# An attention and two-mixer kernel on one core: key chunks of p two per PSUM tile, two-tensor forms of small VectorE operations, q's squares on GpSimd, two score tiles for three

## The chip, the cores and the metric

The kernel runs on one core of one Trainium2 chip. The time is the device time of one execution in microseconds (us). A core has five engines with a queue of instructions each, which run in the order in which they stand: PE (TensorE: matmuls and transposes, its weight loads listed apart as PEld), DVE (VectorE), ACT (ScalarE), POOL (GpSimd) and SP (SyncE, which issues most DMAs here).

## The reference

The input goes through attention (4 batches, 12 heads, 448 tokens, head size 64) and then two mixers on x of 4 x 448 x 768. All of it is float32; the weights of the mixers come as float64.

```
def rmsnorm(x, g):
    rms = sqrt(mean(x * x, axis=-1, keepdims=True) + 1e-06)
    return x / rms * g
q_n, k_n = rmsnorm(q, g_q), rmsnorm(k, g_k)
scores = (q_n @ k_n.T) / sqrt(64)
attn = exp(scores - max(scores)); attn = attn / (sum(attn) + 1e-09)
x = attn @ v                                   # heads side by side: 768 columns
u = x + (x.T @ U @ V).T;            x = u + relu(u @ w_ch1) @ w_ch2        # first mixer
u = x + (relu(x.T @ w_tok1) @ w_tok2).T;  x = u + relu(u @ w_ch1') @ w_ch2'  # second mixer
```

## The kernel before

**Number formats.** Most matmuls split a float32 operand into a high part (fp32r, tiles named `hi`, `ph`, `gh`) and the rest (`lo`, `pl`, `gl`) and add two or three products.

**Attention, head by head.** Heads come in pairs (48 heads, 24 pairs). `load_pair` (L187) fetches q, k and v of a pair, forms the squares of q (ACT, L204) and of k (POOL, L202, by `mul`; on DVE for the first pair), sums them on DVE (L205), and gets 1/rms with a chain of small operations on 112x16 values: L206 on DVE, Ln and Exp on ACT (L208, L209), and a Newton step on DVE (L211 to L214). POOL then scales q and k (L222). Tile `sq` has one buffer, so each square waits for the sum over the one before. `turn_pair` (L233) transposes q and k on PE and splits them; twelve DMAs per pair lay out the operands of the scores.

`softmax` (L267) works on 4 chunks of 112 query rows of a head. For each chunk PE makes a score tile `sc` of 112x448 (two matmuls, one PSUM bank), DVE takes the row maximum `nm` (L276), ACT writes p = exp(sc - max) and the row sum `sm` (L278), and the score tile is free again. After every second chunk DVE adds 1e-9 to two sums (L281) and inverts them (L282), and POOL scales the two chunks of p (L285).

`weigh` (L287) needs all 4 chunks of p of a head. For each of 4 key chunks PE transposes four blocks of p into a PSUM tile `pt` (L304), ACT copies it to `ph` (L312), and DVE computes the rest `pl` (L316). PE adds the products to `pv`, and at the end DVE (with ACT for a split head) writes the result. In the first half of attention the even head of a pair is `whole`: its `ph` is plain float32, it has no `pl`, and its products are float32 matmuls. All other heads are split.

**Stages.** The first 24 heads (batches 0 and 1) run alone, with nothing but a few loads beside them: this is the lone attention. PSUM has 8 banks, and the lone attention gives 3 to `sc`, 1 to `tt` (the turned q and k), and 4 to a pool that `pt` and `pv` share (L550, L551). The other 24 heads run beside the first feed-forward part of the first mixer, with other pools. The rest of the mixers runs without attention. Along with the feed-forward parts, every weight chunk goes through `to_f32` and `split`: ACT L123, DVE L124, L125 and L129, ACT L128, POOL L132, ACT L142, POOL L143.

**What sets the order.** The code says which instruction belongs to which engine; a scheduler that works on a modelled timeline sets the order in each engine's queue when the kernel is built. A change in one stage can so reorder queues all through that stage.

Of the kernel before, what the change touches and what calls it, by code (L numbers as in the profile page):

```python
# [24 lines left out]
def attention_then_two_mixers(  # L25
# [39 lines left out]
    G = 2  # L65
    PAIRS = ((0, 1), (2, 3))

# [30 lines left out]
    pools = {"late": False}  # L98
    AT = dict(qr=2, kr=2, vr=3, qn=1, vs=2, p=8, ph=3, pl=3, sq=1)

# [86 lines left out]
    def load_pair(b, hp, whole, mul):  # L187
# [10 lines left out]
        for i, t in enumerate((qr, kr)):  # L198
            sq = pools["at"].tile([CP, 2 * NC4, D], F32, tag="sq", bufs=AT["sq"], name="sq")
            tt = t.rearrange("p h c d -> p (h c) d")  # L200
            if i:
                mul(sq, tt, tt)  # L202
            else:
                nc.scalar.activation(sq, tt, AF.Square)  # L204
            nc.vector.reduce_sum(ms[:, i], sq, axis=AX.X)  # L205
        nc.vector.tensor_scalar(ms, ms, 1.0 / D, 1e-6, op0=ALU.mult, op1=ALU.add)  # L206
        rs = pools["at"].tile([CP, 2, 8], F32, tag="rs", name="rs")
        nc.scalar.activation(rs, ms, AF.Ln)  # L208
        nc.scalar.activation(rs, rs, AF.Exp, scale=-0.5)  # L209
        nt = pools["at"].tile([CP, 2, 8], F32, tag="nt", name="nt")  # L210
        nc.vector.tensor_mul(nt, rs, rs)  # L211
        nc.vector.tensor_mul(nt, nt, ms)
        nc.vector.tensor_scalar(nt, nt, -0.5, 1.5, op0=ALU.mult, op1=ALU.add)
        nc.vector.tensor_mul(rs, rs, nt)  # L214

# [51 lines left out]
    def softmax(pr, qs, ks, kt):  # L267
        for c in range(NC4):
# [11 lines left out]
            if c % 2:  # L280
                nc.vector.tensor_scalar_add(sm, sm, 1e-9)  # L281
                nc.vector.reciprocal(sm, sm)  # L282
# [5 lines left out]
    def weigh(pr, vj, j, dst, whole):  # L288

        pv = psum("v", [P, S], "pv")  # L290

        def product(kc, ph, pl):
            if whole:
                mm(pv[:D], vj[:, kc], ph, kc == 0, kc == NC4 - 1)
                return
            vk = vj[:, kc].rearrange("p t d -> p (t d)")
            mm(pv, vk, ph, kc == 0, False)
            mm(pv, vk, pl, False, kc == NC4 - 1)

        last = None  # L300
        for kc in range(NC4):
            pt = psum("p", [CP, S], "pt")
            for c in range(NC4):
                nc.tensor.transpose(  # L304
                    pt[:, c * CP:(c + 1) * CP], pr[c][:, kc * CP:(kc + 1) * CP],
                    ident[:CP, :CP],
                )
            if last:
                product(*last)
            ph = pools["pp"].tile([CP, S], F32 if whole else F32R, tag="ph", bufs=AT["ph"],  # L310
                                  name="ph")
            nc.scalar.activation(ph, pt, AF.Copy)  # L312
            pl = None
            if not whole:
                pl = pools["pp"].tile([CP, S], F32R, tag="pl", bufs=AT["pl"], name="pl")
                nc.vector.tensor_sub(pl, pt, f(ph))  # L316
            last = kc, ph, pl
            yield
        product(*last)
# [331 lines left out]
```

## Time and profile before

| | |
|---|---|
| median of 3 runs | 1592.1 us (1589.14 to 1592.72) |
| the profiled execution | 1583.41 us, of which the span of its instructions is 1581.6 us |
| PE busy | 1496.0 us (95%) |
| DVE busy | 1192.7 us (75%) |
| ACT busy | 815.7 us (52%) |
| POOL busy | 847.2 us (54%) |
| mean granted TensorE clock | 0.988 of full speed |

The profiled execution is 8.7 us shorter than the median of the three runs. The lone attention takes about the first 200 us; the 24 heads beside the feed-forward end near 624 us; the mixers alone take the rest. In the rows below, "busy" is the time during which an engine runs at least one instruction, and an arrow `<-` behind an idle time names what ended it.

### The profile page before, as it was taken

To read this page: it belongs to the slowest core of one execution; us is meant where nothing else is said; L and a number is where in the kernel's file an instruction comes from. 1 tells how busy PE (TensorE), PEld (TensorE's weight loads), DVE (VectorE), ACT (ScalarE), POOL (GpSimd) and SP (SyncE) were. 2 spreads that over 40 slices of the span, in tenths; PEclk is the share of its full clock that TensorE was granted. 3 is DMA by queue.
4 is the path that set the end of the run, shared out by engine and by line. 5 is a ranking of instruction groups with operands and counts; after the bars stand their busy time and mean duration, and the time that the engine had idled before them with its cause. 6 is when DMAs were issued, how large, how long until landed. Compare 5 with 4: busy or idle time off the path is not lost.

```text
span 1581.6 us, 21878 instructions
## 1 busy us (share of the span) xinstructions
PE 1496.0 (95%) x7648; PEld 1303.0 (82%) x7648; DVE 1192.7 (75%) x1981; ACT 815.7 (52%) x1511; POOL 847.2 (54%) x645
## 2 busy tenths in 40 slices
PE   5999978999999999999999999999999999999998
PEld 3565566888788899898898988889999998998997
DVE  6899888988897887667858677677676676748663
ACT  5888765666566665434534345344344343524431
POOL 4667656666666554544745454455455453535540
PEclk9999979999999999999999999999999999999999
DMA  6656533445434422323314334233333332203312
GB/s 154 155 154 165 149 130 113 127 130 157 144 112 139 116 92 83 122 91 113 120 43 137 101 100 150 66 116 133 101 101 120 100 110 90 80 13 120 128 61 71
DMA packets 116046, 178.22 MB, mean 113 GB/s; under 512 B 9248, under 2 KB 105984, under 8 KB 115936
## 3 DMA queue, kind: packets, MB, share of 16 engines
q1 hardware_dynamic: 115616, 176.82, 36.7%
q8 instruction: 61, 1.00, 0.3%
q14 instruction: 49, 0.40, 0.1%
q10 hardware_dynamic: 320, 0.00, 0.0%
HBM read 135.50 MB, written 8.26 MB: 91 GB/s over the span
## 4 chain that ended last, share of the span: by engine, by line
PE 62%; DVE 12%; POOL 4%; DMA 4%; ACT 3%; issue 2%; SPq 0%; DVEq 0%; POOLq 0%; ACTq 0%
PE ps_x L77 27%; PE ps_g L77 25%; DVE w_bits L124 3%; DVE w_bits L129 2%; PE ps_u L77 2%; PE ps_t L77 2%; POOL w L143 2%; PE pv L77 2%; DMA qs<-hi 2%; DMA w_raw<-in_moe_w_ch_dram 1%; POOL w_bits L132 1%; DVE w_bits L125 1%; PE sc L77 1%; PE pt L304 1%; DVE xT L478 1%
## 5 line engine op out<-in xcount | busy, mean ns | idle before, releaser
L77 PE MATMUL ps_x<-gs,w 128*128 128x448 f32 x2592 | 566.5, 370 | 22.1 <-DVE xT L478 11.5
L77 PE MATMUL ps_g<-u,w 128*128 128x448 f32 x2592 | 546.4, 367 | 1.6 <-DVE gs L465 0.9
L77 PEld LDWEIGHTS ps_x<-gs,w 128*128 128x128 f32 x2592 | 483.4, 190 | 71.5 <-DVE xT L478 18.0
L77 PEld LDWEIGHTS ps_g<-u,w 128*128 128x128 f32 x2592 | 484.1, 188 | 42.2 <-DVE gs L465 1.5
L132 POOL TENSOR_TENSOR w_bits<-w_bits,w_round 128x768 uint32<-128x768 uint32 (+2 forms) x152 | 279.8, 1841 | 270.7 <-DVE w_bits L129 211.9
L143 POOL TENSOR_TENSOR w<-w_bits,w 128x768 fp32r<-128x768 f32 (+3 forms) x154 | 285.9, 1866 | 199.2 <-ACT w L142 198.9
L478 DVE TENSOR_TENSOR xT<-ps_x,xT 128x448 f32<-128x448 f32 x432 | 265.9, 619 | 121.4 <-PE ps_x L77 119.6
L128 ACT ACTIVATE w_round<-w_raw 128x768 uint32<-128x768 uint32 (+2 forms) x152 | 135.2, 889 | 186.2 <-POOL w_bits L132 186.0
L124 DVE TENSOR_SCALAR w_bits<-w_bits 128x768 f32<-128x768 f32 (+2 forms) x152 | 145.3, 956 | 96.0 <-ACT w_bits L123 95.9
L142 ACT ACTIVATE w<-w_bits 128x768 fp32r<-128x768 f32 (+3 forms) x154 | 124.8, 830 | 124.0 <-PE ps_x L77 68.0
L285 POOL TENSOR_SCALAR p<-p,sm 112x448 f32<-112x448 f32 x192 | 129.0, 685 | 95.3 <-DVE sm L282 49.0
L123 ACT ACTIVATE w_bits<-w_raw 128x768 f32<-128x768 f32 (+2 forms) x152 | 135.3, 891 | 85.5 <-POOL w L143 77.7
L129 DVE SCALAR_TENSOR_TENSOR w_bits<-w_raw,w_bits 128x768 uint32<-128x768 uint32 (+2 forms) x152 | 168.7, 1110 | 2.1
L278 ACT ACTIVATE p<-sc,nm 112x448 f32<-112x448 f32 x192 | 121.9, 637 | 49.8 <-DVE nm L276 41.9
L125 DVE TENSOR_SCALAR w_bits<-w_bits 128x768 uint32<-128x768 uint32 (+2 forms) x152 | 137.7, 906 | 2.9
L464 ACT ACTIVATE gs<-ps_g 128x448 fp32r<-128x448 f32 x144 | 77.8, 543 | 108.8 <-PE ps_g L77 106.1
L465 DVE SCALAR_TENSOR_TENSOR gs<-ps_g,gs 128x448 fp32r<-128x448 f32 x144 | 88.9, 619 | 52.8 <-ACT gs L464 52.5
L276 DVE TENSOR_REDUCE nm<-sc 112x1 f32<-112x448 f32 x192 | 116.3, 613 | 8.4 <-PE sc L77 7.8
L304 PEld LDWEIGHTS pt<-ident,p 112*112 112x112 f32 x768 | 86.7, 134 | 41.5 <-issue 18.5
L312 ACT ACTIVATE ph<-pt 112x448 fp32r<-112x448 f32 (+1 forms) x192 | 101.3, 546 | 30.2 <-PE pt L304 29.0
L304 PE MATMUL pt<-ident,p 112*112 112x112 f32 x768 | 111.4, 262 | 5.2 <-DVE pl L316 2.6
L387 POOL TENSOR_TENSOR u<-xT,u 128x448 fp32r<-128x448 f32 x48 | 59.1, 1248 | 65.5 <-ACT u L386 65.5
(74 smaller groups left out, 1438.4 us busy)
## 6 DMA issues: line engine op xcount, KB each, us to landing
w_raw<-in_moe_w_ch_dram SPq DMA_DIRECT2D x144, 768.0 KB, 4.4
ks<-hi SPq DMA_DIRECT2D x96, 112.0 KB, 2.4
kt<-lo SPq DMA_DIRECT2D x96, 112.0 KB, 2.3
qr<-in_q_dram SPq DMA_DIRECT2D x24, 224.0 KB, 3.1
kr<-in_k_dram SPq DMA_DIRECT2D x24, 224.0 KB, 3.2
vr<-in_v_dram SPq DMA_DIRECT2D x24, 224.0 KB, 3.1
qs<-hi SPq DMA_DIRECT2D x48, 112.0 KB, 2.8
qs<-lo SPq DMA_DIRECT2D x48, 112.0 KB, 2.7
```

What stands on the lines that cost most here:

```text
L77: nc.tensor.matmul(o, lhsT=l, rhs=r, start=start, stop=stop)
L123: nc.scalar.activation(f(w), f(high), AF.Abs)
L124: nc.vector.tensor_scalar_max(f(w), f(w), TINY)
L125: nc.vector.tensor_scalar(w, w, 3, 0x3FFFFFF8, op0=ALU.logical_shift_left, op1=ALU.bitwise_and)
L128: nc.scalar.activation(r, low, AF.Copy, scale=2.0 ** -29)
L129: nc.vector.scalar_tensor_tensor(w, high, 0xC0000000, w, op0=ALU.bitwise_and, op1=ALU.bitwise_or)
L132: nc.gpsimd.tensor_tensor(w, w, r, op=ALU.add)
L142: nc.scalar.activation(hi, w, AF.Copy)
L143: nc.gpsimd.tensor_sub(lo, w, f(hi))
L285: nc.gpsimd.tensor_scalar(x, x, sm[:, i:i + 1], 1.0, op0=ALU.mult, op1=ALU.mult)
L304: nc.tensor.transpose(pt[:, c * CP:(c + 1) * CP], pr[c][:, kc * CP:(kc + 1) * CP], ident[:CP, :CP],)
L478: nc.vector.tensor_add(xT[:, dc], px, xT[:, dc])
```

## The change

Five things change, all in attention.

- **Two key chunks per tile.** In the lone attention `weigh` turns two key chunks into one `pt` tile of two banks. One ACT copy and one DVE subtraction then cover 112x896 where there were two of 112x448. `ph` and `pl` have two buffers of double width for four of single width. Beside the feed-forward one chunk per tile remains (`turn=1`).
- **PSUM of the lone attention.** Score tiles go from 3 to 2, `pt` gets 2 tiles of two banks, and `pv` gets a bank of its own.
- **Two-tensor forms.** L206 and L281 were `tensor_scalar` with two constants or one; they become `scalar_tensor_tensor` with a constant tile (`eps`, `zeros`) as second tensor.
- **Newton step.** The operations L211 to L214 become three: the factor -0.5 goes into the first, and the addition of 1.5 into the last.
- **q's squares** are made by `mul` like k's: on POOL, for the first pair on DVE.

```diff
+    zeros = const.tile([P, 2], F32, name="zeros")
+    nc.vector.memset(zeros, 0.0)
+    eps = const.tile([P, 16], F32, name="eps")
+    nc.vector.memset(eps, 1e-6)
...
-            if i:
-                mul(sq, tt, tt)
-            else:
-                nc.scalar.activation(sq, tt, AF.Square)
+            mul(sq, tt, tt)
             nc.vector.reduce_sum(ms[:, i], sq, axis=AX.X)
-        nc.vector.tensor_scalar(ms, ms, 1.0 / D, 1e-6, op0=ALU.mult, op1=ALU.add)
-        rs = pools["at"].tile([CP, 2, 8], F32, tag="rs", name="rs")
+        ms = ms.rearrange("p a b -> p (a b)")
+        nc.vector.scalar_tensor_tensor(
+            ms, ms, 1.0 / D, eps[:CP], op0=ALU.mult, op1=ALU.add)
+        rs = pools["at"].tile([CP, 16], F32, tag="rs", name="rs")
...
-        nc.vector.tensor_mul(nt, rs, rs)
+        nc.vector.scalar_tensor_tensor(nt, rs, -0.5, rs, op0=ALU.mult, op1=ALU.mult)
         nc.vector.tensor_mul(nt, nt, ms)
-        nc.vector.tensor_scalar(nt, nt, -0.5, 1.5, op0=ALU.mult, op1=ALU.add)
-        nc.vector.tensor_mul(rs, rs, nt)
+        nc.vector.scalar_tensor_tensor(rs, nt, 1.5, rs, op0=ALU.add, op1=ALU.mult)
...
-                nc.vector.tensor_scalar_add(sm, sm, 1e-9)
+                nc.vector.scalar_tensor_tensor(
+                    sm, sm, 1e-9, zeros[:CP], op0=ALU.add, op1=ALU.add)
...
+        def product(kcs, ph, pl):
+            for i, kc in enumerate(kcs):
+                if whole:
+                    mm(pv[:D], vj[:, kc], ph[:, i], kc == 0, kc == NC4 - 1)
+                    continue
+                vk = vj[:, kc].rearrange("p t d -> p (t d)")
+                mm(pv, vk, ph[:, i], kc == 0, False)
+                mm(pv, vk, pl[:, i], False, kc == NC4 - 1)
...
+        n = AT["turn"]
+        for k0 in range(0, NC4, n):
+            kcs = range(k0, k0 + n)
+            pt = psum("p", [CP, n, BANK], "pt")[:, :, :S]
+            for i, kc in enumerate(kcs):
+                for c in range(NC4):
+                    nc.tensor.transpose(
+                        pt[:, i, c * CP:(c + 1) * CP], pr[c][:, kc * CP:(kc + 1) * CP],
+                        ident[:CP, :CP],
+                    )
             if last:
                 product(*last)
...
-        AT.update(p=12, ph=4, pl=4)
-        open_pools(inner, (("pp", 1, 0), ("s", 3, 1), ("t", 1, 1), ("p", 4, 1)))
-        pools["v"] = pools["p"]
+        AT.update(p=12, ph=2, pl=2, turn=2)
+        open_pools(inner, (("pp", 1, 0), ("s", 2, 1), ("t", 1, 1), ("p", 2, 1), ("v", 1, 1)))
...
-        AT.update(p=8, ph=3, pl=3)
+        AT.update(p=8, ph=3, pl=3, turn=1)
```

The queues change all through attention and are the same from the mixers without attention on. Three places follow. In the names, a number after a tile tells one allocation from the next; the line numbers of the changed kernel are up to 11 higher.

PE, in the middle of the lone attention, before: the transposes of the head whose chunks are p_1982, p_1999, p_2022 and p_2040, with the score matmuls and the products between them.

```order
L304 MATMUL pt_2136<-ident_67,p_1982 112x112
L304 MATMUL pt_2136<-ident_67,p_1999 112x112
L304 MATMUL pt_2136<-ident_67,p_2022 112x112
L304 MATMUL pt_2136<-ident_67,p_2040 112x112
L77 MATMUL sc_2258<-ks_2083,qs_2080 112x448
L77 MATMUL sc_2258<-kt_2086,qs_2080 112x448
L77 MATMUL sc_2351<-ks_2092,qs_2089 112x448
L77 MATMUL sc_2351<-kt_2095,qs_2089 112x448
L77 MATMUL pv_1984<-pl_2033,vs_1455 128x448
```

PE, at the like place now: the transposes of the head whose chunks are p_1861, p_1882, p_1894 and p_1918, from the first two chunks on.

```order
L314 MATMUL pt_2004<-ident_67,p_1861 112x112
L314 MATMUL pt_2004<-ident_67,p_1882 112x112
L77 MATMUL sc_2027<-ks_1755,qs_1752 112x448
L77 MATMUL sc_2027<-kt_1758,qs_1752 112x448
L77 MATMUL sc_2047<-ks_1755,qs_1752 112x448
L77 MATMUL sc_2047<-kt_1758,qs_1752 112x448
L77 MATMUL pv_1863<-pl_1911,vs_1374 128x448
L77 MATMUL pv_1863<-ph_1909,vs_1374 128x448
L77 MATMUL pv_1863<-pl_1911,vs_1374 128x448
L314 MATMUL pt_2034<-ident_67,p_1861 112x112
L314 MATMUL pt_2034<-ident_67,p_1882 112x112
```

Before, sc_2258 and sc_2351 are the last chunk of the head two further on and the first of the head after that. Now sc_2027 and sc_2047 are the third and fourth chunk of the very next head, and the head's transposes begin with its first two chunks, into both double tiles, ahead of the other two.

POOL, in the lone attention, before: the square of k between chunks of p.

```order
L222 TENSOR_TENSOR kn_2122<-kr_2100,rs_2112 112x2x4x64
L202 TENSOR_TENSOR sq_2331<-kr_2323 112x512
L285 TENSOR_SCALAR p_1945<-p_1945,sm_1939 112x448
L285 TENSOR_SCALAR p_1960<-p_1960,sm_1939 112x448
L143 TENSOR_TENSOR vs_1678<-vr_1656,vs_1678 112x4x64
L285 TENSOR_SCALAR p_1982<-p_1982,sm_1976 112x448
```

POOL, at the like place now: both squares, k's of one pair and q's of the next.

```order
L291 TENSOR_SCALAR p_1655<-p_1655,sm_1649 112x448
L291 TENSOR_SCALAR p_1676<-p_1676,sm_1649 112x448
L206 TENSOR_TENSOR sq_2183<-kr_2175 112x512
L206 TENSOR_TENSOR sq_2386<-qr_2379 112x512
L291 TENSOR_SCALAR p_1688<-p_1688,sm_1682 112x448
L148 TENSOR_TENSOR vs_1580<-vr_1559,vs_1580 112x4x64
```

A second square now stands ahead of the scaling of p_1688, and it waits for DVE's sum over the first.

## Rows read from the trace of the kernel before

**Rows 1.** Busy time by stretch: from:to, length, then each engine (instructions), clock, DMA.

```profile
core 0: us, PE busy (x) PEld busy (x) DVE busy (x) ACT busy (x) POOL busy (x), PEclk, DMA share, GB/s
39.00:188.00 149.00, 139.17 (x733) 86.96 (x732) 137.80 (x340) 123.77 (x334) 100.65 (x135) 0.99 0.62 157
203.00:624.00 421.00, 394.35 (x2101) 345.49 (x2102) 366.73 (x648) 262.42 (x535) 253.12 (x215) 0.97 0.41 121
```

**Rows 2.** Line 321, once per pair: durations, then first and last start.

```profile
L321 DVE COPY xT<-pv x12: 604/606/617, 38.6 to 197.6; 64x448 f32<-64x448 f32 x12
```

**Rows 3.** Waits of PE's weight loads, 39 to 188 us: total, times, longest.

```profile
PEld sc L77 <- ACT p L278: 6.1, 13, 0.8
PEld pv L77 <- ACT ph L312: 5.0, 9, 1.0
PEld pt L304 <- POOL p L285: 2.9, 3, 1.5
PEld sc L77 <- ACT sq L204: 2.1, 2, 1.4
```

**Rows 4.** Groups on DVE, 39 to 188 us: count | busy, mean ns | idle before.

```profile
L276 DVE TENSOR_REDUCE nm<-sc 112x1 f32<-112x448 f32 x83 | 50.0, 613 | 2.7 <-PE sc L77 2.4
L316 DVE TENSOR_TENSOR pl<-pt,ph 112x448 fp32r<-112x448 f32 x40 | 24.0, 607 | 0.0
...
L281 DVE TENSOR_SCALAR sm<-sm 112x2 f32<-112x2 f32 x41 | 10.8, 263 | 1.4 <-ACT p L278 1.3
...
L206 DVE TENSOR_SCALAR ms<-ms 112x16 f32<-112x16 f32 x13 | 5.2, 397 | 0.0
L212 DVE TENSOR_TENSOR nt<-nt,ms 112x16 f32<-112x16 f32 x12 | 4.6, 383 | 0.1
L214 DVE TENSOR_TENSOR rs<-rs,nt 112x16 f32<-112x16 f32 x12 | 4.1, 345 | 0.1
L211 DVE TENSOR_TENSOR nt<-rs 112x16 f32<-112x16 f32 x12 | 3.3, 272 | 0.3 <-ACT rs L209 0.3
L213 DVE TENSOR_SCALAR nt<-nt 112x16 f32<-112x16 f32 x12 | 3.2, 264 | 0.1
```

**Rows 5.** Groups on ACT and POOL, the same stretch.

```profile
L278 ACT ACTIVATE p<-sc,nm 112x448 f32<-112x448 f32 x83 | 52.9, 642 | 6.2 <-DVE nm L276 3.8 <-PE pt L304 1.1 <-DVE sm L282 1.1
L285 POOL TENSOR_SCALAR p<-p,sm 112x448 f32<-112x448 f32 x83 | 52.4, 646 | 28.9 <-DVE sm L282 8.2 <-ACT ph L312 7.4 <-PE pt L304 6.9
...
L312 ACT ACTIVATE ph<-pt 112x448 fp32r<-112x448 f32 x40 | 21.1, 554 | 6.0 <-PE pt L304 6.0
...
L202 POOL TENSOR_TENSOR sq<-kr 112x512 f32<-112x512 f32 x13 | 13.7, 1051 | 5.1 <-DMA kr<-in_k_dram 1.5 <-DVE ms L205 1.5 <-DVE sm L281 1.4
...
L204 ACT ACTIVATE sq<-qr 112x512 f32<-112x512 f32 x13 | 8.3, 639 | 2.7 <-DMA qr<-in_q_dram 2.6
```

**Rows 6.** The narrower evictions of 384 columns, whole execution.

```profile
L380 DVE TENSOR_TENSOR xs<-pt_x,xs 112x384 fp32r<-112x384 f32 x64 | 34.0, 550 | 13.1 <-ACT xs L379 12.9
L379 ACT ACTIVATE xs<-pt_x 112x384 fp32r<-112x384 f32 x64 | 29.9, 488 | 18.3 <-PE pt_x L372 17.8
```

**Rows 7.** DVE and POOL in order of time, near 294 and 452 us: start, length.

```profile
294.26 4.30 DVE L206 TENSOR_SCALAR ms<-ms 112x16 f32<-112x16 f32 x1
294.89 3.64 POOL L143 TENSOR_TENSOR w<-w_bits,w 128x768 fp32r<-128x768 f32 x2
...
451.19 1.36 POOL L202 TENSOR_TENSOR sq<-kr 112x512 f32<-112x512 f32 x1
451.68 3.48 DVE L129 SCALAR_TENSOR_TENSOR w_bits<-w_raw,w_bits 128x768 uint32<-128x768 uint32 x1
452.51 1.84 POOL L143 TENSOR_TENSOR w<-w_bits,w 128x768 fp32r<-128x768 f32 x1
```

**Rows 8.** The chain that ended last, two of its pieces: start, length, what.

```profile
240.31 6.32 DVE w_bits L124
...
273.33 3.62 DVE nt L213
```

More of the change, by code (lines that the diff above doesn't have):

```diff
@@ L65, in attention_then_two_mixers @@
     G = 2
-    PAIRS = ((0, 1), (2, 3))
+    BANK = 512
     const = ctx.enter_context(tc.tile_pool(name="const", bufs=1))
@@ L98, in attention_then_two_mixers @@
     pools = {"late": False}
-    AT = dict(qr=2, kr=2, vr=3, qn=1, vs=2, p=8, ph=3, pl=3, sq=1)
+    AT = dict(qr=2, kr=2, vr=3, qn=1, vs=2, p=8, ph=3, pl=3, sq=1, turn=1)
     def open_pools(stack, side):
@@ L200, in load_pair @@
             tt = t.rearrange("p h c d -> p (h c) d")
-            if i:
-                mul(sq, tt, tt)
-            else:
-                nc.scalar.activation(sq, tt, AF.Square)
+            mul(sq, tt, tt)
             nc.vector.reduce_sum(ms[:, i], sq, axis=AX.X)
-        nc.vector.tensor_scalar(ms, ms, 1.0 / D, 1e-6, op0=ALU.mult, op1=ALU.add)
-        rs = pools["at"].tile([CP, 2, 8], F32, tag="rs", name="rs")
+        ms = ms.rearrange("p a b -> p (a b)")
+        nc.vector.scalar_tensor_tensor(
+            ms, ms, 1.0 / D, eps[:CP], op0=ALU.mult, op1=ALU.add)
+        rs = pools["at"].tile([CP, 16], F32, tag="rs", name="rs")
         nc.scalar.activation(rs, ms, AF.Ln)
         nc.scalar.activation(rs, rs, AF.Exp, scale=-0.5)
-        nt = pools["at"].tile([CP, 2, 8], F32, tag="nt", name="nt")
-        nc.vector.tensor_mul(nt, rs, rs)
+        nt = pools["at"].tile([CP, 16], F32, tag="nt", name="nt")
+        nc.vector.scalar_tensor_tensor(nt, rs, -0.5, rs, op0=ALU.mult, op1=ALU.mult)
         nc.vector.tensor_mul(nt, nt, ms)
-        nc.vector.tensor_scalar(nt, nt, -0.5, 1.5, op0=ALU.mult, op1=ALU.add)
-        nc.vector.tensor_mul(rs, rs, nt)
+        nc.vector.scalar_tensor_tensor(rs, nt, 1.5, rs, op0=ALU.add, op1=ALU.mult)
+        rs = rs.rearrange("p (a b) -> p a b", a=2)
         def scale(i, shape):
@@ L290, in weigh @@
         pv = psum("v", [P, S], "pv")
[L292 to L298, printed above, removed]
-        last = None
[L301 to L307, printed above, removed]
+        def product(kcs, ph, pl):
[6 more added lines that the diff above has]
+                mm(pv, vk, pl[:, i], False, kc == NC4 - 1)
+        last = None
+        n = AT["turn"]
[8 more added lines that the diff above has]
+                    )
             if last:
                 product(*last)
-            ph = pools["pp"].tile([CP, S], F32 if whole else F32R, tag="ph", bufs=AT["ph"],
+            ph = pools["pp"].tile([CP, n, S], F32 if whole else F32R, tag="ph", bufs=AT["ph"],
                                   name="ph")
@@ L314, in weigh @@
             if not whole:
-                pl = pools["pp"].tile([CP, S], F32R, tag="pl", bufs=AT["pl"], name="pl")
+                pl = pools["pp"].tile([CP, n, S], F32R, tag="pl", bufs=AT["pl"], name="pl")
                 nc.vector.tensor_sub(pl, pt, f(ph))
-            last = kc, ph, pl
-            yield
+            last = kcs, ph, pl
+            for _ in kcs:
+                yield
         product(*last)
```

## The prediction

> **What bounds the kernel now.** I read the table of busy time by stretch first, to see which stages the edits can reach. Nothing is edited in the mixers without attention, and the queues there keep their order, so their time is taken as unchanged. Two stages remain. In the middle of the lone attention PE is busy 139.2 of 149 us and DVE 137.8; ACT has 123.8 and POOL 100.7 [rows 1]. PE and DVE are both within 8% of full, and neither alone explains the time. The line that runs once per pair of heads starts 12 times between 38.6 and 197.6 us, so a pair takes (197.6 - 38.6) / 11 = 14.45 us [rows 2]. Beside the feed-forward (421 us) PE is busy 394.4 us, that is 94%, and DVE 366.7, that is 87% [rows 1]: there PE sets the end and DVE matters where PE waits for it.
>
> Next I read what PE waits for in the lone stage. The largest waits of its weight loads are for a free score tile, 6.1 us in 13 waits behind ACT's exponential; for `ph` from ACT, 5.0 us; for p from POOL, 2.9 us; and 2.1 us behind q's square on ACT [rows 3]. So the lone stage is a chain of four engines that hand work over with little room, and what counts is both how much work DVE and ACT have and how far ahead each is.
>
> **The change part by part, lone attention.** There are 12 pairs; the first is start-up, so I count 11.
>
> *Wider `pl`.* DVE's subtraction of 448 columns takes 607 ns [rows 4], the one of 384 takes 550 ns [rows 6]. That is 57 / 64 = 0.89 ns per column, so one of 896 should take 607 + 448 x 0.89 = 1006 ns. A pair has four `pl` (one split head): 4 x 607 - 2 x 1006 = 0.42 us less on DVE. The least it can be is nothing, if the wide one takes 2 x 607.
>
> *Newton step.* The five small operations take 397 + 272 + 383 + 264 + 345 = 1661 ns per pair [rows 4]. Four at the mean of 332 take 1329: 0.33 us less. The long means are waits for POOL, shown below.
>
> *Two-tensor forms.* L281 takes 263 ns for two columns and L206 397 ns for 16 [rows 4]; nearly all of it is not work. The rows show why: at 294.26 us L206 takes 4.30 us and ends as POOL ends a pair of `w` operations that began at 294.89 and took 3.64 [rows 7]. Two-tensor forms do the same: L212 and L214 have no constant in place of a tensor and average 383 and 345 ns; at 451.68 us a scalar_tensor_tensor over SBUF takes 3.48 us behind a POOL square and a POOL subtraction in a row [rows 7]. So I count the forms at nothing. If they did help, rival C has the price.
>
> *q's squares.* ACT loses 639 ns per pair and POOL gains 1051 [rows 5]. The wider `ph`: 554 ns for 448 columns [rows 5], 488 for 384 [rows 6], so 1.03 ns per column and 1016 for 896; four wide ones for eight save 8 x 554 - 4 x 1016 = 0.37 us. ACT is relieved by 1.0 us per pair, which takes away the 2.1 us behind q's square [rows 3], and part of the 5.0. POOL goes from 100.7 to 100.7 + 10.3 x 1.05 = 111.5 of 149 us, still the least busy but in the way: more of DVE's small operations will find it running. With 7% more POOL time the waits inside the 1.33 + 2.1 us of small operations per pair grow by some 0.1 us.
>
> *Sum of the work.* DVE: 0.42 + 0.33 - 0.1 = 0.65 us per pair. PE's own idle time is 149 - 139.2 = 9.8 us, or 0.95 us per pair, so the period can follow DVE that far: 11 x 0.65 = 7 us gained. ACT's relief is counted inside this, since ACT is less full than DVE; the bound of both is PE's idle time, 11 x 0.95 = 10.5 us.
>
> *Two score tiles and a shorter lead.* This costs, and the trace has no row for two tiles. From below: nothing, if exponentials come in time. From above: the 6.1 us per 149 [rows 3] doubled, 6.1 x 159 / 149 = 6.5 us more. The order of the queue shows a second loss. Before, when PE begins to transpose a head in the second half of the stage, it has issued seven chunks of later heads; now at most two, in every head. I take a third of the upper end, 2 us, because only short waits (0.8 us at most) stand there now.
>
> *A bank of its own for `pv`.* The next head's first product waits until DVE has read the last head's `pv` (606 ns at L321 [rows 2]). In the new order a dozen transposes and two score chunks stand between, so this costs nothing; without that cover it would be 0.6 us per head.
>
> Lone attention: 7 - 2 = 5 us gained.
>
> **Beside the feed-forward.** Seven or so pairs run their small operations here. One operation fewer saves 7 x 0.33 = 2.3 us of DVE, mostly hidden under PE; q's squares add 7 x 1.05 = 7.4 us of POOL time. The long DVE waits there (L124 6.32 us, L213 3.62 us, both in the final chain [rows 8]) are meetings of two queues: L124 is not edited, and the order of POOL before it now holds one square more. L213's operation is gone, but its successors can meet POOL as well. I count 1 us of gain, with -8 to +7 for meetings that vanish or come anew.
>
> Total 6 us: 1583.4 to 1577.4 for the profiled execution. That execution is 8.7 us under the median, so on the median 1592.1 - 6 = **1586 us**.
>
> **The rivals.** *A, the lead is lost (slower).* The chain from a score tile to a transposable p is 613 (maximum) + 642 (exponential) + 263 (sum) + 2 x 646 (POOL, two chunks) = 2.8 us without any queueing [rows 4, 5]. A lead of two chunks is half a head: 14.45 / 2 / 2 = 3.6 us. One square ahead of p on POOL (1.05 us) eats what is left, and the new order has two in a row there, the second waiting for DVE's sum over the first. If every split or whole head then waits 0.6 us or more on PE, 22 heads x 0.6 = 13 us go, against 7 gained: 6 us slower, 1598; at 1.0 us per head, 15 slower, 1607. It decides from 0.3 us per head. For it: the queue's order, and PE's waits for p of up to 1.5 us already with the long lead [rows 3]. Against it: POOL idles a third of the time [rows 1].
>
> *B, no difference.* Saved DVE time turns into DVE waiting for score tiles; 7 against 5 to 9 lost: 1592 within 3.
>
> *C, two-tensor forms are served sooner.* The longest DVE waits, 4.30, 3.62 and 6.32 us, are all on one-tensor forms [rows 7, 8]. If the new forms waited for no more than one POOL operation, L206's 4.30 and L213's 3.62 us would shrink to the rest of one, about half of 1.84 us [rows 7], and PE would get back most of 4.30 + 3.62 - 1.84 = 6.1 us beside the feed-forward: 1592.1 - 6 - 6 = 1580. Against it stands the 3.48 us two-tensor wait [rows 7]. The Trainium skill (SBUF — State Buffer, section on SBUF's two separate sides) says that a DVE operation with two SBUF inputs contends with a GpSimd operation that reads SBUF, and that whichever starts first holds the shared ports for one whole instruction. By that rule the wait would end with the POOL operation in flight, which is this rival; the 3.48 us wait, which outlasts the POOL square and the next subtraction, does not agree.
>
> **How the numbers follow.** The forecast (3.2 to 10 us faster) has a chance of 0.40, C 0.10, B 0.18, A 0.32. The other signs hold half, so the forecast's own range is 1582 to 1589; the range that should hold 8 in 10 reaches from 1576 (C with its meetings) to 1603 (A at 0.8 us per head). About 0.2%, 3.2 us, is what a measurement can tell from no change. Faster: 0.40 + 0.10 = 0.50; same 0.18; slower 0.32.
>
> **What would show it.** Right: `pl` and `ph` of 896 columns near 1.0 us each; the stretch of the lone attention shorter by about 5 us, with DVE's busy time per pair down by 0.65 us; the new forms with means of 250 to 400 ns as now. Rival A: PE's weight loads waiting for p from POOL far above 2.9 us, and waits for score tiles above 6.1. Rival C: the new forms near their shortest. The prediction is wrong outright if the wide operations cost twice the narrow ones, or if a new long DVE wait falls where PE has nothing else.

## The result and the profile after

The changed kernel takes **1609.6 us** (median; 1604.98 to 1610.01), the kernel before 1590.8 beside it: ratio **1.0111**, 95% interval 1.0088 to 1.0134. It is 18.8 us slower; the forecast was 1586, the range ended at 1603.

The place is found with two marks. The first is the last run of the line that evicts a split head's `pv`, for `xT`: the end of the lone attention. The second is the first matmul into `ps_t`, the first token mixing, from which on PE's queue is the same in every kernel here. Each line gives instruction, count, min/median/max in ns, and first and last start; of the kernel before (L325) and of the changed one (L336):

```profile
L325 DVE TENSOR_TENSOR xT<-pv,tmp x12: 617/619/619, 49.5 to 203.5; 64x448 f32<-64x448 f32 x12
...
L77 PE MATMUL ps_t<-xs,w x192: 333/336/445, 736.4 to 1397.6; 112*128 112x384 f32 x192
```

```profile
L336 DVE TENSOR_TENSOR xT<-pv,tmp x12: 618/619/619, 47.5 to 228.7; 64x448 f32<-64x448 f32 x12
...
L77 PE MATMUL ps_t<-xs,w x192: 331/336/443, 761.1 to 1424.2; 112*128 112x384 f32 x192
```

The lone attention ends 25.2 us later (203.5 to 228.7), and at the second mark the delay is 24.7 us (736.4 to 761.1). So the whole loss is made in the first 230 us; beside the feed-forward nothing is gained or lost. These two executions are 26.6 us apart, where the medians are 18.8 apart: the profiled one of before ran 7.4 us under the median beside it. Before, a pair took 14.45 us [rows 2]; after, the line that answers starts from 35.2 to 216.6, so (216.6 - 35.2) / 11 = 16.5 us:

```profile
L332 DVE COPY xT<-pv x12: 596/616/617, 35.2 to 216.6; 64x448 f32<-64x448 f32 x12
```

Busy time by stretch, as in [rows 1] (stretch, length, then each engine with its instructions, clock, DMA):

```profile
39.00:188.00 149.00, 129.42 (x657) 80.50 (x655) 118.65 (x263) 100.14 (x244) 95.48 (x126) 0.98 0.54 132
225.00:648.00 423.00, 393.12 (x2101) 346.54 (x2102) 371.14 (x641) 258.42 (x526) 264.93 (x221) 0.97 0.42 120
```

In the lone attention every engine is less busy than before: PE 129 of 149 us for 139, DVE 119 for 138, ACT 100 for 124, POOL 95 for 101. No engine became the bound, and the granted clock, 0.98 for 0.99, did not do it either: 6.8 of the 149 us ran at the lower level (1.2 GHz), 3.4 before. Something makes all four wait. PE's weight loads in that stretch, as in [rows 3] (waiting for <- released by: total, times, longest):

```profile
PEld sc L77 <- ACT p L283: 20.1, 36, 1.5
...
PEld pv L77 <- DVE pl L326: 8.9, 11, 2.4
PEld pv L77 <- ACT ph L322: 6.5, 11, 1.4
...
PEld pt L314 <- POOL p L291: 3.6, 5, 1.1
```

The wait for a free score tile went from 6.1 us in 13 waits to 20.1 in 36. The wait for p from POOL, which rival A named, went from 2.9 to 3.6 only. The wait for `pl` grew too, to 8.9 us; before it was

```profile
PEld pv L77 <- DVE pl L316: 3.2, 5, 0.9
```

The operations themselves, as in [rows 4, 5] (DVE, then ACT; count | busy, mean ns | idle before):

```profile
L281 DVE TENSOR_REDUCE nm<-sc 112x1 f32<-112x448 f32 x74 | 45.1, 615 | 8.6 <-PE sc L77 7.5
L326 DVE TENSOR_TENSOR pl<-pt,ph 112x896 fp32r<-112x896 f32 x18 | 19.4, 1080 | 1.0 <-ACT ph L322 1.0
...
L286 DVE SCALAR_TENSOR_TENSOR sm<-sm,zeros 112x2 f32<-112x2 f32 x36 | 8.7, 242 | 10.7 <-ACT p L283 10.5
L209 DVE SCALAR_TENSOR_TENSOR ms<-ms,eps 112x16 f32<-112x16 f32 x9 | 5.0, 556 | 0.2
L218 DVE SCALAR_TENSOR_TENSOR rs<-nt,rs 112x16 f32<-112x16 f32 x9 | 4.5, 503 | 0.1
```

```profile
L283 ACT ACTIVATE p<-sc,nm 112x448 f32<-112x448 f32 x73 | 46.4, 639 | 25.4 <-DVE nm L281 21.5 <-POOL sq L206 3.4 <-DVE sm L286 0.3
L322 ACT ACTIVATE ph<-pt 112x896 fp32r<-112x896 f32 x19 | 17.2, 916 | 8.5 <-PE pt L314 8.5
```

The wide operations are what was forecast: `pl` 1080 ns (two narrow ones 1214), `ph` 916 (two narrow ones 1108). But ACT, which waited 3.8 us for maxima [rows 5], now waits 21.5, and DVE waits 7.5 us for scores where it waited 2.4 [rows 4]. PE waits for ACT, ACT for DVE, DVE for PE: a ring with too few tiles in it.

One turn of the ring, from the trace of the changed kernel in order of time (start, length, engine, line, what, idle before):

```profile
105.77 0.62 DVE L281 TENSOR_REDUCE nm<-sc 112x1 f32<-112x448 f32 x1
...
106.31 0.68 DVE L207 TENSOR_REDUCE ms<-sq 112x8 f32<-112x512 f32 x1
...
106.65 0.43 PE L77 MATMUL sc<-ks,qs 128*112 128x448 f32 x1
...
106.80 1.36 POOL L148 TENSOR_TENSOR w<-w_bits,w 128x448 fp32r<-128x448 f32 x1
106.93 0.37 PE L77 MATMUL sc<-kt,qs 128*112 128x448 f32 x1
107.02 2.17 DVE L209 SCALAR_TENSOR_TENSOR ms<-ms,eps 112x16 f32<-112x16 f32 x1
107.31 0.63 ACT L283 ACTIVATE p<-sc,nm 112x448 f32<-112x448 f32 x1
...
108.12 1.04 POOL L206 TENSOR_TENSOR sq<-qr 112x512 f32<-112x512 f32 x1
...
109.12 0.61 DVE L281 TENSOR_REDUCE nm<-sc 112x1 f32<-112x448 f32 x1
...
109.86 0.62 ACT L283 ACTIVATE p<-sc,nm 112x448 f32<-112x448 f32 x1
```

The chunk whose scores begin at 106.65 needs 0.65 us of matmuls, 0.61 of maximum and 0.62 of exponential. Its tile is held until 110.48, 3.8 us, because its maximum stands in DVE's queue behind a sum and behind L209, which ends only as POOL's second operation does. That second operation is q's square, which the change put there; the run h1 below shows that the end does not depend on it. With two tiles, one such hold leaves PE a single tile to go on with.

### The profile page after: what moved, and what is told of

It reads as the page before. It is cut to its first block, busy times and chain, and to the rows that moved or that the text cites. A ratio compares the mean times of both kernels' runs of the same rounds, so it can differ in the third digit from the quotient of the medians.

```text
span 1608.2 us, 21731 instructions
## 1 busy us (share of the span) xinstructions
PE 1504.6 (94%) x7648; PEld 1311.9 (82%) x7648; DVE 1199.0 (75%) x1936; ACT 799.7 (50%) x1439; POOL 875.2 (54%) x668
## 4 chain that ended last, share of the span: by engine, by line
PE 66%; DVE 16%; POOL 6%; ACT 6%; issue 4%; DMA 3%; SPq 0%; ACTq 0%; DVEq 0%; POOLq 0%
PE ps_x L77 26%; PE ps_g L77 25%; PE pv L77 4%; DVE w_bits L129 3%; PE sc L77 3%; POOL w_bits L137 2%; PE pt L314 2%; POOL w L148 2%; DVE w_bits L134 2%; PE ps_u L77 2%; DVE nm L281 2%; DVE xT L489 2%; DVE w_bits L130 2%; DVE pl L326 1%; PE ps_t L77 1%
## 5 line engine op out<-in xcount | busy, mean ns | idle before, releaser
L77 PE MATMUL ps_x<-gs,w 128*128 128x448 f32 x2592 | 569.0, 371 | 19.7 <-DVE xT L489 10.3
L129 DVE TENSOR_SCALAR w_bits<-w_bits 128x768 f32<-128x768 f32 (+2 forms) x152 | 147.1, 968 | 95.5 <-ACT w_bits L128 95.4
L134 DVE SCALAR_TENSOR_TENSOR w_bits<-w_raw,w_bits 128x768 uint32<-128x768 uint32 (+2 forms) x152 | 162.3, 1068 | 2.2
L130 DVE TENSOR_SCALAR w_bits<-w_bits 128x768 uint32<-128x768 uint32 (+2 forms) x152 | 141.4, 930 | 2.9
L281 DVE TENSOR_REDUCE nm<-sc 112x1 f32<-112x448 f32 x192 | 116.2, 614 | 11.8 <-PE sc L77 10.5
L322 ACT ACTIVATE ph<-pt 112x448 fp32r<-112x448 f32 (+2 forms) x144 | 94.0, 668 | 31.5 <-PE pt L314 31.1
L77 PE MATMUL sc<-ks,qs 128*112 128x448 f32 x192 | 83.1, 434 | 22.0 <-ACT p L283 16.3
```

What stands on the lines that cost most here:

```text
L77: nc.tensor.matmul(o, lhsT=l, rhs=r, start=start, stop=stop)
L129: nc.vector.tensor_scalar_max(f(w), f(w), TINY)
L130: nc.vector.tensor_scalar(w, w, 3, 0x3FFFFFF8, op0=ALU.logical_shift_left, op1=ALU.bitwise_and)
L134: nc.vector.scalar_tensor_tensor(w, high, 0xC0000000, w, op0=ALU.bitwise_and, op1=ALU.bitwise_or)
L281: nc.vector.tensor_reduce(nm, sc, axis=AX.X, op=ALU.max, negate=True)
```

## The experiments

The theories: **1**, two score tiles make the loss; **2**, the two-chunk turn makes it, by coarser hand-over of `pt`, `ph` and `pl`; **3**, q's squares on POOL make it. Times are medians, ratios are against the kernel before, measured beside each. The stages: "lone" to the end of the 24th eviction of `pv`, "mixed" from there to the first `ps_t` matmul, "common" from there to the end of the span, all of the one profiled execution.

| kernel | median us | ratio (95%) | lone | mixed | common |
|---|---|---|---|---|---|
| before | 1589.6 to 1593.3 | 1 | 204.1 | 532.2 | 845.2 |
| before again | 1588.2 | one run | 205.6 | 532.1 | 848.8 |
| after | 1609.6 | 1.0111 (1.0088 to 1.0134) | 229.3 | 531.8 | 847.1 |
| e3, two score tiles | 1608.6 | 1.0121 (1.0082 to 1.0160) | 234.0 | 529.0 | 845.2 |
| e2, all of the PSUM part | 1611.6 | 1.0149 (1.0107 to 1.0191) | 231.7 | 531.8 | 847.1 |
| e1, all but the PSUM part | 1590.9 | 1.0019 (1.0000 to 1.0039) | 203.4 | 536.2 | 848.5 |
| e7, after with three shared tiles | 1607.1 | 1.0102 (1.0064 to 1.0140) | 215.7 | 541.5 | 848.5 |
| f2, before with three shared tiles | 1612.1 | 1.0130 (1.0096 to 1.0164) | 221.5 | 540.6 | 847.9 |
| f5, four score tiles | 1604.5 | 1.0089 (1.0068 to 1.0109) | 214.7 | 539.2 | 848.3 |
| f1, shorter lead | 1597.1 | 1.0041 (1.0021 to 1.0061) | 211.3 | 533.6 | 852.9 |
| x1, no maximum, three tiles | 1567.1 | 0.9851 (0.9826 to 0.9875) | 191.9 | 523.1 | 852.9 |
| x2, no maximum, two tiles | 1564.9 | 0.9845 (0.9803 to 0.9888) | 200.7 | 512.7 | 845.9 |
| g1, squares on POOL | 1592.0 | 1.0001 (0.9979 to 1.0023) | 204.9 | 537.4 | 851.8 |
| g2, Newton step | 1578.5 | 0.9917 (0.9886 to 0.9948) | 203.3 | 524.9 | 849.5 |
| f6, forms and Newton | 1579.3 | 0.9932 (0.9908 to 0.9956) | 203.9 | 525.7 | 854.6 |
| f6b, the same again | 1576.5 | 0.9916 (0.9883 to 0.9948) | 202.5 | 525.4 | 847.0 |
| h1, after with squares on ACT | 1609.2 | 1.0108 (1.0077 to 1.0139) | 229.5 | 529.8 | 848.5 |

The two profiles of before agree within 1.5 us up to the second mark, and the common stage, the same work everywhere, scatters from 845 to 855. So lone and mixed are what to read; the common stage is scatter.

### Which part makes the loss

**e3**, one number:

```diff
-        open_pools(inner, (("pp", 1, 0), ("s", 3, 1), ("t", 1, 1), ("p", 4, 1)))
+        open_pools(inner, (("pp", 1, 0), ("s", 2, 1), ("t", 1, 1), ("p", 4, 1)))
```

> The kernel before with one edit: score tiles 3 to 2 in the lone attention. Everything else is as before, and one PSUM bank then lies idle. In the profile of the changed kernel PE's weight loads wait 25.5 us for a score tile behind the exponential (46 waits, at most 1.5 us) between 20 and 220 us, before 7.5 us in 16. Theory 1 (the two score tiles make nearly the whole loss, since scores can no longer run ahead of the exponential): 1605 to 1612, 15 to 21 us slower than before, with over 20 us of such waits. Theory 2 (the two-chunk turn makes it: pt, ph and pl are handed over half as often, and PE waits for pl): this run is 1591 to 1595, since the prediction's 2 us for the tiles then holds. Theory 3 (q's squares on POOL make it): 1591 to 1595 too.

Measured: 1608.6 us, 1.0121. This single edit costs as much as the whole change. Its waits for a score tile, 39 to 188 us, with the kernel's name for the exponential:

```profile
PEld sc L77 <- ACT p L278: 14.4, 19, 1.8
```

They more than double, from 6.1 [rows 3]; between 20 and 220 us they come to 17.3 us, under the 20 that theory 1 had named. Busy time in that stretch, as in [rows 1], and its wait for `pl`:

```profile
39.00:188.00 149.00, 133.77 (x644) 80.27 (x643) 120.53 (x299) 110.36 (x290) 86.82 (x117) 0.93 0.53 134
```

```profile
PEld pv L77 <- DVE pl L316: 4.2, 6, 1.0
```

The granted clock is 0.93, a mean of stretches at 2.4 and at 1.2 GHz, where the changed kernel has 0.98. In the whole lone stage 26.2 us ran at 1.2 GHz, 5.8 before. Half of the difference, 10 us, is the most that this can have added to the lone stage of e3's profile; the changed kernel lost its 25 us almost without it.

**e2**, the kernel before with the diff of `weigh` and of the pools; small operations and squares stay.

> The kernel before with only the PSUM part of the change: two key chunks per tile of pt, ph and pl, two score tiles, pv in a bank of its own; the small operations and the place of q's squares as before. Theory 1 and theory 2 both expect the loss here, 1605 to 1612 (theory 1 as much as in the run that has the two score tiles alone; theory 2 over 10 us more than that run). Theory 3: 1588 to 1594.

Measured: 1611.6 us, 1.0149. That is 3.0 us more than e3 in the median, and 2.3 us less in the lone stage (231.7 against 234.0), so the wide turn adds nothing that shows, where theory 2 wanted over 10 us. PE does wait longer for `pl` than in e3, from 39 to 188 us:

```profile
PEld pv L77 <- DVE pl L325: 7.8, 11, 1.8
```

So the coarser hand-over is there, but it is not the loss. Theory 2 falls here.

**e1**, the other half: the changed kernel with

```diff
-        AT.update(p=12, ph=2, pl=2, turn=2)
-        open_pools(inner, (("pp", 1, 0), ("s", 2, 1), ("t", 1, 1), ("p", 2, 1), ("v", 1, 1)))
+        AT.update(p=12, ph=4, pl=4, turn=1)
+        open_pools(inner, (("pp", 1, 0), ("s", 3, 1), ("t", 1, 1), ("p", 4, 1)))
+        pools["v"] = pools["p"]
```

> The changed kernel with the PSUM tiles of before: one key chunk per tile, three score tiles, pv sharing the four banks of pt. What is left of the change are the two-tensor forms, the shorter Newton step and q's squares on POOL. Theories 1 and 2: 1586 to 1592, no loss, or the few us that the prediction counted for the Newton step. Theory 3: 1602 to 1610, with POOL's squares waiting for DVE's sum as in the changed kernel (9.9 us in 8 waits between 20 and 220 us).

Measured: 1590.9 us, 1.0019; lone 203.4 as before. Theory 3 falls for the lone attention. That there is no gain either is taken up below.

### Tiles or turn: other splits of the eight banks

**e7** gives the changed kernel three score tiles, by letting the transposes of q and k use them too:

```diff
-        open_pools(inner, (("pp", 1, 0), ("s", 2, 1), ("t", 1, 1), ("p", 2, 1), ("v", 1, 1)))
+        open_pools(inner, (("pp", 1, 0), ("s", 3, 1), ("p", 2, 1), ("v", 1, 1)))
+        pools["t"] = pools["s"]
```

> The changed kernel with three score tiles again: the transposes of q and k take turns in the score tiles, so the eight banks are three for scores, four for two wide pt, one for pv. Theory 1: most of the loss goes, 1588 to 1595, and waits for a score tile fall under 12 us between 20 and 220 us. Theory 2: 1603 to 1610, with PE's waits for pl still near 11 us in that stretch. Theory 3: 1603 to 1610 too.

Measured: 1607.1 us, 1.0102. A miss for theory 1 as I had put it: the waits for a score tile still come to 20.6 us between 20 and 220 us, where it named under 12. It needed a partner with one chunk per tile, **f2**:

```diff
-        open_pools(inner, (("pp", 1, 0), ("s", 3, 1), ("t", 1, 1), ("p", 4, 1)))
-        pools["v"] = pools["p"]
+        open_pools(inner, (("pp", 1, 0), ("s", 3, 1), ("p", 4, 1), ("v", 1, 1)))
+        pools["t"] = pools["s"]
```

> The kernel before, one key chunk per tile, with three score tiles that the transposes of q and k share, and pv in a bank of its own beside four for pt: the partner of the run with three shared score tiles and the wide turn, which took 1607.1. Theory 2 (there the wide turn made the loss): 1588 to 1594 here. Theory 1 (the shared tiles are worth little more than two of their own, since two transposed tiles per pair hold a score tile too): 1602 to 1609 here.

Measured: 1612.1 us, 1.0130. Without the wide turn the loss is there as well, in fact 5.8 us more of it in the lone stage (221.5 against 215.7). So the loss of e7 in the lone stage needs no wide turn; sharing the tiles is enough. That a tile which waits for a split of q or k is a score tile less would explain it, but no run shows this by itself. Only part of the loss is in the lone stage: the mixed stage, where nothing was edited, takes 541.5 and 540.6 us for 532.2. In its first 60 us the granted clock is 0.74 in both, 0.82 and 0.79 in the two profiles of before; why is open.

The wide turn's own gain is not shown. The lone stage is 2.3 us shorter in e2 than in e3 and 5.8 us shorter in e7 than in f2. But e2 and e7 also spent 6.0 and 10.3 us less of it at 1.2 GHz than their partners, which is worth up to 3 and 5 us, and each pair differs by more than the turn (`pv`'s bank; the small operations). Three score tiles of their own beside the wide turn were not run: with two wide `pt`, one `tt` and one `pv` they would need 3 + 4 + 1 + 1 = 9 banks.

**f5** goes the other way:

```diff
-        open_pools(inner, (("pp", 1, 0), ("s", 3, 1), ("t", 1, 1), ("p", 4, 1)))
+        open_pools(inner, (("pp", 1, 0), ("s", 4, 1), ("t", 1, 1), ("p", 3, 1)))
```

> The kernel before with four score tiles and three tiles for pt and pv in place of three and four. Theory 1: what PE still waits for a score tile (7.5 us between 20 and 195 us) shrinks, 1580 to 1588, unless pt and pv, now one tile fewer, take it back. Theory 2 (the hand-over of pt to ph and pl limits): slower, 1594 to 1602.

Measured: 1604.5 us, 1.0089; a miss for theory 1 again, and slower than theory 2 had it. Of the loss, 7 us lie in the mixed stage (539.2), with the same clock of 0.74 at its start. Its waits from 39 to 188 us:

```profile
PEld sc L77 <- ACT p L278: 9.4, 18, 1.0
PEld pv L77 <- DVE pl L316: 7.4, 14, 1.1
PEld pv L77 <- ACT ph L312: 7.2, 14, 1.7
PEld pt L304 <- ACT ph L312: 6.5, 7, 2.1
```

Transposes now wait for a free `pt` (6.5 us), and products for `pl`. The exponentials come later too: a chunk's wait between maximum and exponential is 2.7 us on average (1.0 before), so the fourth tile only holds chunks that ACT does not get to. Three and four was the best split of those tried; a bank taken from either side costs 14 to 19 us.

### Why two tiles are too few

With fewer tiles the scheduler also lets scores run less far ahead. **f1** shortens that lead with all three tiles kept:

```diff
-        AT.update(p=12, ph=4, pl=4)
+        AT.update(p=8, ph=4, pl=4)
```

> The kernel before with 8 buffers of p for 12 in the lone attention, all three score tiles kept. Scores may then run ahead of the transposes by two heads at most, where the queue of before lets them run up to nearly three; what stands between a head's scores and its transposes shrinks by about a third in PE's queue. Two score tiles alone cost 19 us (1608.6 against 1589.6). Theory 1a (the loss comes from score tiles as such: a chunk's round through maximum and exponential holds a tile for 3.3 us, and PE waits when two are held): this run is 1588 to 1593, unchanged, with waits for a score tile near 7.5 us between 20 and 195 us. Theory 1b (the loss comes from the lead that scores have over the transposes, which three tiles let the scheduler build): 1595 to 1605, at least a third of the loss.

Measured: 1597.1 us, 1.0041, in the range of theory 1b. When PE begins to transpose a head it has now issued at most three chunks of later heads (seven before, two in the changed kernel). The lone stage is 7.2 us longer, about a quarter of what two tiles cost there; in the median it is 6.1 us, a third. This is not the lead alone. The exponential writes p, and with fewer buffers of p it begins 2.25 us after its maximum on average (1.0 before), so f1 also holds its score tiles longer (table below). Nor is the lead as short as with two tiles. So a shorter lead costs at most 7 us in this form, and something else is worth more.

**x1** and **x2** settle what: the row maximum is left out, with three tiles and with two.

```diff
-            nm = pools["at"].tile([CP, 1], F32, tag="nm", bufs=8, name="nm")
-            nc.vector.tensor_reduce(nm, sc, axis=AX.X, op=ALU.max, negate=True)
...
-            nc.scalar.activation(p, sc, AF.Exp, bias=nm, accum_out=sm[:, c % 2:c % 2 + 1])
+            nc.scalar.activation(p, sc, AF.Exp, bias=flat[:CP], accum_out=sm[:, c % 2:c % 2 + 1])
```

> The kernel before without the row maximum: DVE's 192 maxima are left out, the exponential takes a bias of zero. The hold of a score tile loses the maximum (0.61 us) and most of the wait ahead of it (0.63 us), of 3.27 us. DVE loses 4.9 us per pair in the lone attention, so PE, idle 9.8 of 149 us there, sets the end: lone attention 152 to 162 us between the first and the 24th pv (164.9 before); total 1570 to 1585.

> The same without the row maximum, and with two score tiles for three. (a) The hold decides: at about 2.0 us per chunk, 8 chunks hold 16 us per pair of the 28.9 us that two tiles give, 55%, about as full as three tiles were (61%); the run is then within 6 us of its partner with three tiles, against 19 us with the maximum. (b) The shorter lead of the order decides: it stays 15 us or more slower than its partner, since scores stand no further ahead of the transposes than in the run with two tiles and the maximum.

Measured: 1567.1 and 1564.9 us, 0.9851 and 0.9845, intervals overlapping. (x1's lone attention, 155 us from the first to the 24th `pv`, is in its range, the total 3 us under it.) In the medians the third tile is worth 19 us with the maximum, and nothing without it. The lone stage up to the 23rd eviction of `pv` ends at 186.6 and 187.4 us (before 198.2, e3 220.7); so the 22 us that two tiles cost up to there shrink to 1. The last head of x2 is late by 8 us, as that of e3 is by 7: this part stays without the maximum, and x2 makes it up in the mixed stage, which is shorter by 10 us for a reason that these profiles do not place. Waits for a score tile in x2, 39 to 188 us:

```profile
PEld sc L77 <- ACT ph L312: 4.2, 6, 0.7
PEld sc L77 <- ACT p L278: 3.2, 6, 1.0
```

In x2 the lead of the queue is two or three chunks of later heads, for the most part, as in e3; so without the maximum a short lead does no harm. What differs is the hold of a tile, from a chunk's first score matmul to the end of its exponential, averaged over the 77 to 81 chunks from 39 us to between 170 and 200 us:

| kernel | hold, us | us per chunk | tiles held, of |
|---|---|---|---|
| before | 3.82 | 1.81 | 2.11 of 3 |
| after | 3.17 | 2.06 | 1.54 of 2 |
| e3 | 3.02 | 2.09 | 1.45 of 2 |
| x1 | 2.73 | 1.66 | 1.65 of 3 |
| x2 | 1.87 | 1.72 | 1.09 of 2 |
| f1 | 4.8 | 1.86 | 2.6 of 3 |
| f5 | 5.5 | 1.87 | 2.9 of 4 |

(The 3.3 us of some expectations came from a coarser pairing of matmuls and maxima, which misses part of the queueing; the argument is the same.) Of the 3.82 us before, 0.77 go to the two matmuls, 0.78 to waiting for the maximum, 0.61 to the maximum, 1.01 to waiting for the exponential and 0.64 to the exponential. Before, all three tiles are held for 37% of the time; in the changed kernel both are held for 64% of it. This share is no price by itself: in f1 all three are held for 65% of the time, and it lost 6 us. The runs show that the loss up to the 23rd head goes away with the maximum. They do not part the two ways in which it acts, the shorter hold and a DVE with 4.9 us less to do per pair, since a busy DVE is itself much of the hold. Without the maximum DVE is far from full, as these rows of x1 and x2 show (as in [rows 1]; 137.8 of 149 us before):

```profile
39.00:180.00 141.00, 137.43 (x753) 88.52 (x751) 99.20 (x257) 121.90 (x333) 100.96 (x137) 1.00 0.64 165
39.00:180.00 141.00, 137.32 (x750) 88.23 (x748) 101.22 (x257) 123.27 (x334) 98.47 (x132) 1.00 0.65 168
```

### The small operations

**g2**, the Newton step alone:

```diff
-        nc.vector.tensor_mul(nt, rs, rs)
+        nc.vector.scalar_tensor_tensor(nt, rs, -0.5, rs, op0=ALU.mult, op1=ALU.mult)
         nc.vector.tensor_mul(nt, nt, ms)
-        nc.vector.tensor_scalar(nt, nt, -0.5, 1.5, op0=ALU.mult, op1=ALU.add)
-        nc.vector.tensor_mul(rs, rs, nt)
+        nc.vector.scalar_tensor_tensor(rs, nt, 1.5, rs, op0=ALU.add, op1=ALU.mult)
```

> The kernel before with only the Newton step shortened (three operations for four); the one-tensor operations on the mean squares and on the sums stay as before. The queues then have nearly the order of the run with forms and Newton step, so the difference of the two is the forms. Prediction's term (0.33 us per pair, forms at nothing): 1579 to 1587, most of the 11 us. Rival C (the two-tensor forms are served sooner beside POOL): 1586 to 1591, the gain being the forms'.

Measured: 1578.5 us, 0.9917. **f6** has the two-tensor forms as well:

> The kernel before with only the two-tensor forms and the shorter Newton step; q's squares stay on ACT, and PSUM stays as before. The run with the squares on POOL as well took 1590.9, 1.0019 of before. If the prediction's terms hold (0.33 us per pair of DVE time, forms at nothing): 1583 to 1588, 2 to 6 us faster. If DVE's small operations cost the end nothing: 1588 to 1592. If q's squares on POOL cost nothing either: as the run with them, 1589 to 1593.

Measured: 1579.3 us, 0.9932. (One of its eight executions took 6334 us; it is not in the ratio, and without it the median is 1577.2.) Once more as **f6b**:

> The kernel before with only the two-tensor forms and the shorter Newton step, a second time with more rounds: 1576 to 1584, 0.990 to 0.996 of before, if the gain holds.

Measured: 1576.5 us, 0.9916. So the Newton step gains 0.7 to 0.8%, the forms add nothing, and the medians of g2 and f6 lie below the ranges that the prediction's terms gave them. Of the gain, 7 us lie in the mixed stage (525 for 532) and one or two in the lone one; the rest is not placed by these profiles. The forms' waits show why they add nothing. In f6b the two-tensor form that replaces L206 (L212 there) waits beside POOL's queue as L206 did near 294 us, 4.07 us for 4.30 [rows 7]:

```profile
291.37 4.07 DVE L212 SCALAR_TENSOR_TENSOR ms<-ms,eps 112x16 f32<-112x16 f32 x1
```

```profile
290.77 1.05 POOL L230 TENSOR_TENSOR qn<-qr,rs 112x512 f32<-112x512 f32 x1
291.77 3.64 POOL L148 TENSOR_TENSOR w<-w_bits,w 128x768 fp32r<-128x768 f32 x2
```

So does the first operation of the Newton step, two-tensor over 16 columns (its like takes 262 ns on average in the lone attention of g2):

```profile
388.63 3.76 DVE L219 SCALAR_TENSOR_TENSOR nt<-rs 112x16 f32<-112x16 f32 x1
```

```profile
388.70 3.66 POOL L148 TENSOR_TENSOR w<-w_bits,w 128x768 fp32r<-128x768 f32 x2
```

Each ends as the second of two POOL operations of `w` ends, not the first, and each began while a shorter POOL operation ahead of these two was in flight (to 291.82 and to 388.74). The Trainium skill (SBUF — State Buffer, section on SBUF's two separate sides) says that whichever starts first holds the shared ports for one whole instruction. If the engine that waits came next after that, L212 would go on at 291.82, when the operation in flight ends; the trace does not agree, since it lasts to 295.44.

**g1**, q's squares alone:

```diff
-            if i:
-                mul(sq, tt, tt)
-            else:
-                nc.scalar.activation(sq, tt, AF.Square)
+            mul(sq, tt, tt)
```

> The kernel before with only q's squares moved from ACT to POOL. The run with the forms and the Newton step took 1579.3 (0.9932 of before), the run that has the squares on POOL as well 1590.9 (1.0019): 14 us apart. If the squares cost by themselves (POOL's queue: two squares in a row hold up the scaling of p, and a square waits for DVE's sum over the one before): 1598 to 1606. If they cost only together with the new forms, or the order in which the queues were built cost it: 1588 to 1594. The prediction itself put them at 0 to 2 us.

Measured: 1592.0 us, 1.0001. Alone they cost nothing that shows. Together with forms and Newton step (e1) they leave nothing of that gain: mixed 536.2 us for 525.5. Summing what DVE's instructions in the mixed stage take above the lower quartile of their kind (same line, operands and shape) gives 68 us for f6b, 70 for g2, 72 and 75 for before, 77 for g1, 85 for e1. That fits longer meetings with POOL, but each of these kernels also has another order of its queues, and no run here parts the two. This stays open.

**h1**, the changed kernel with the lines of g1 put back:

> The changed kernel with q's squares back on ACT, all else as changed. If the squares cost 14 us in this company too: 1594 to 1600. If PE's waits for score tiles hide what POOL does: 1605 to 1611, as the changed kernel.

Measured: 1609.2 us, 1.0108; lone 229.5 as with the squares on POOL (229.3). In the changed kernel they cost and gain nothing.

**b2**, the kernel before, unchanged:

> The kernel before, unchanged, for a second profiled execution. If its first profile is typical: 204 us to the end of the 24th pv, 532 us from there to the first token-mixing matmul, 845 us from there to the end. If the scatter lies in the common tail, the last number alone is larger, by up to 8 us.

Measured: 1588.2 us; 205.6, 532.1 and 848.8. The scatter is in the common stage and a little in the lone one.

## Why the prediction was wrong

**The step that failed** is the price of two score tiles: "I take a third of the upper end, 2 us, because only short waits (0.8 us at most) stand there now." The run with that edit alone lost 19 us in the median, 28 to 30 in the lone stage of its profile (234.0 against 204.1 and 205.6), up to 10 of which can be the clock. Even the upper end, 6.5 us, was no bound: doubling the wait that three tiles leave says nothing about two. A warning was in the trace of before. A chunk holds its tile for 3.82 us there, a pair has 8 chunks, so 30.6 us of tile time per pair; two tiles offer 2 x 14.45 = 28.9 us. At the old pace they do not suffice even with no gap between two holds; the pace has to fall, or the holds have to shrink, and in the changed kernel both did (16.5 us per pair, 3.17 us per hold). It is no exact bound, since much of a hold is queueing, which is less with fewer tiles. I had worked out an unqueued chain of 2.8 us, sum and scaling included, and held it against PE's lead over the transposes instead of against the tiles.

**Rival A** had the sign and its upper case the size, 1607, but not the place: PE's wait for p from POOL grew by 0.7 us, its wait for score tiles by 14. A lead cut to three chunks costs 7 us of lone attention at most (f1), and in x2, without the maximum, a short one does no harm. **Rival B** named DVE's wait for scores, which did grow (2.4 to 7.5 us), and put the loss too low.

**The wide operations** were near. `pl` was put at 1006 ns and took 1080, `ph` at 1016 and took 916. So a wide `pl` saves 0.13 us, not 0.21, and 11 pairs with two of them 3 us of DVE time. What of this reaches the end is not shown; the pairs of runs above differ by 2 and 6 us of lone attention, and most of that can be the clock. The prediction's list of PE's waits passes over those for `pl`, 3.2 us, which grew to 8.9. It was paid for with a bank that was worth more.

**The Newton step** had the right sign and was mis-sized: 3.6 us lone and 1 us mixed of the sum, where the runs show 12 to 16 in the median (g2, f6, f6b), 7 of it placed in the mixed stage. The meetings with POOL that vanish or come anew, which I had left at -8 to +7 us, may be the larger part of it: DVE's excess over the lower quartile is 2 to 7 us less in these runs than in before. But the order of the queues changed as well, and no run parts the two.

**The forms at nothing** held (f6b against g2: 0.9916 and 0.9917); rival C fell with the 4.07 us wait above. The means of 250 to 400 ns that were to be a sign did not come in the changed kernel: L209 takes 556 and L218 503 in the rows above. **q's squares** at 0.1 us per pair fit the runs g1 and h1, where they cost nothing that shows, and not e1, beside the Newton step. **`pv`'s own bank at nothing** was not tried by itself.

**Beside the feed-forward**, 531.8 us after against 532.2 before: 1 us of gain was forecast, 0.4 is there. The chain that ended last still passes two long DVE waits, as in [rows 8] (start, length, what). L129 is L124 of before; L217 is the product of the Newton step that was two-tensor before as well:

```profile
263.62 5.33 DVE w_bits L129
...
294.45 2.79 DVE nt L217
```

## What to carry to other kernels

Before taking a buffer from a ring of engines, multiply the mean hold of one buffer, queueing included, by the number of uses per period, and compare it with buffers times period: if what is left would not hold the work (106% here, with a loss), the buffer may not be spare, however short the waits on it look while it is there. At 82% the buffer was spare (x1's 8 x 2.73 us against two tiles at 13.3 us per pair). The sum warns and does not prove: a hold with queueing grows where chunks only stand and wait, as in f5, whose four tiles at 5.5 us would call three too few, though before, with three (and one more for `pt` and `pv`), is faster. A bank that buys fewer, wider operations is worth what those save, and here that was far less than what the bank earned as a score tile. Try a bundle's parts alone: this one held a gain of 0.8% that the rest covered.

## What was not expected of the hardware

A small DVE operation's wait beside POOL is a matter of the moment, even in one and the same program. In the first profile of before, L206 takes 4.30 us near 294 us [rows 7]; in the second, the same operation of the same queue met POOL elsewhere:

```profile
296.44 0.91 DVE L206 TENSOR_SCALAR ms<-ms 112x16 f32<-112x16 f32 x1
297.26 1.88 DVE L281 TENSOR_SCALAR sm<-sm 112x2 f32<-112x2 f32 x1
```

```profile
296.27 1.03 POOL L222 TENSOR_TENSOR qn<-qr,rs 112x512 f32<-112x512 f32 x1
297.28 1.83 POOL L143 TENSOR_TENSOR w<-w_bits,w 128x768 fp32r<-128x768 f32 x1
```

These two, L206 in [rows 7], L209 in the turn of the ring and the two of f6b above all end within 0.05 us of the end of a POOL operation. For L206 here it is the one in flight when it began (297.35 and 297.30), although the next follows at once; for L281 and L209 it is the second, for the other three the third. Yet the mixed stage took 532.2 and 532.1 us. A wait of 3.4 us more or less on DVE left no trace at its end, so one long wait in one profile, even in the middle of the stage that matters, is no price.
